# Transposing P by a product with the diagonal of reciprocal sums, in the first twelve units of a fused attention and MLP kernel

## The chip, the core and the metric

The kernel runs on one NeuronCore of one Trainium2 chip. A core has five engines with their own instruction queues: TensorE (PE) for matrix products, VectorE (DVE), ScalarE (ACT), GpSimd (POOL), and SyncE (SP), which here only starts transfers. Each engine works its queue in order. An instruction waits at the head of its queue until what it needs has been signalled by the others, and everything behind it waits with it. The metric is the device time of one execution in microseconds (us). The kernel before took 779.98 us, the median of three runs (778.26 to 780.73).

## The reference

The reference is three steps on float32 data, one after the other: attention with 32 global and 512 local tokens over batch 4 and 8 heads, a gated feed-forward block with a convolution over three tokens, and an FFT mixing block with layer norm and a second feed-forward. The change lies in the local attention of the first step:

```python
s_ll = scale * np.matmul(q_l, k_l.transpose(0, 1, 3, 2))     # 512 x 512 per batch and head
s_ll = np.where(|q - k| <= 32, s_ll, -1e9)
s_lg = scale * np.matmul(q_l, k_g.transpose(0, 1, 3, 2))     # 512 x 32
s_l = np.concatenate([s_lg, s_ll], axis=-1)
e = np.exp(s_l - max)                                        # sm(s)
a_l = e / (np.sum(e, axis=-1, keepdims=True) + 1e-9)
out_l = np.matmul(a_l, np.concatenate([v_g, v_l], axis=2))
```

The weights of the feed-forward block, `w_in` (512 x 1024) and `w_out` (1024 x 512), arrive as float64 bit patterns. The kernel turns each into a pair of 32-bit values, a rounded high part and a low part that is the rest.

## The kernel before

**Units.** Local attention is cut into 32 units. A unit is one pair of heads and one half of the 512 queries of one batch: two heads times two blocks of 128 queries, so four blocks of 128 queries, each against a band of 224 key columns. The steps of unit i, with the names that the order uses:

- `S` (PE): scores of the four blocks, into two PSUM banks.
- `M` (DVE, four): scale, add the mask, take the row's extreme, write the block of P to SBUF (`pb`, 128 x 224 of 256 columns; the last 32 are zero).
- `E` (ACT, four): exponential in place, with the row sums.
- `A` (ACT) and `R` (DVE): add 1e-9 to the four sums, take the reciprocals (`sm`, columns 12 to 15).
- `N` (POOL, four): scale each block of P by its reciprocals, in place (`s_scale`).
- `T` (PE, two halves, one per head): transpose the two blocks of the half, each in two pieces of 128 columns, with `pe.transpose` (`t_mm`).
- `C` (DVE for half 0, ACT for half 1): copy the transposed half to SBUF (`t_evac`).
- `V` (PE): multiply by the values (`pv_mm`), eight products with 64 columns of the values stationary, written alternately to the lower and the upper 64 partitions of the output.
- `XH` (ACT) and `XL` (DVE): the output as a rounded high part and a low part.

Beside them run the global tokens' attention (`GS` to `GXL`), the feed-forward of the first batch (`F`, `H`, `Y`, `TH`, `B`, `D`, where `F` is the product with `w_in` and `D` that with `w_out`), and the making of the sixteen weight tiles, number k of which takes `lw` (SP, load 512 KB), `wa` (ACT, magnitude), `wc` (POOL, clamp), `wt` (ACT) or `wu` (DVE) for the tail bits, `ws` and `wo` (DVE, join and sign), `wh` (ACT, the high part) and `wl` (DVE, the low part, `w_low`).

**Order.** For the first thirteen units the order of all engines is written out by hand in the table `PLAN`: every word is one step, and each engine gets its steps in the order of the words. `PLAN` ends before S13. From unit 13 on, loops give the order on PE and SP, and a scheduler that goes by priorities gives it on the other three engines. Unit 12 has its scores and scaling in `PLAN` and its transposes in the loop.

**Buffers.** P lies in three pairs of `pb` buffers in turn. The transposed halves of units 0, 2, 4 and 6 go to the PSUM banks a2 and a3; those of all others go to the banks s and t, which most scores use too (those of units 1, 3, 5 and 7 use a0 and a1).

Of the kernel before, what the change touches and what calls it, by code (L numbers as in the profile page):

```python
# [42 lines left out]
PLAN = """
lg lq0 lw0 lm1 lq1 li lv0 lw1 S0 lm0 lq2 lc lq3 wu0 wa0 lv1 M0.0 wc0 M0.1 E0.0 M0.2 E0.1 M0.3 S1 ws0 E0.2 E0.3 wo0 A0 lw2 R0 M1.0 wh0 N0.0 lw3 M1.1
E1.0 lq4 wl0 N0.1 E1.1 M1.2 N0.2 M1.3 T0.0 E1.2 E1.3 N0.3 C0.0 wa1 T0.1 wt1 wc1 A1 C0.1 S2 R1 ws1 N1.0 ca wo1 N1.1 V0 lq5 M2.0 wh1 N1.2 M2.1 E2.0 M2.2
wl1 N1.3 E2.1 T1.0 M2.3 E2.2 cd T1.1 E2.3 A2 S3 C1.1 C1.0 wa2 R2 N2.0 V1 wt2 M3.0 M3.1 E3.0 N2.1 M3.2 M3.3 E3.1 N2.2 wu3 lv2 T2.0 XH0 lq6 E3.2 N2.3
XL0 E3.3 C2.0 wc2 T2.1 A3 wa3 R3 S4 ws2 N3.0 C2.1 wo2 N3.1 V2 lw4 M4.0 wh2 N3.2 M4.1 lw5 E4.0 M4.2 N3.3 lw6 wl2 E4.1 T3.0 lw7 M4.3 E4.2 wc3 C3.0 T3.1
E4.3 A4 ws3 S5 C3.1 R4 wo3 wa4 N4.0 V3 M5.0 wh3 N4.1 M5.1 M5.2 E5.0 N4.2 M5.3 E5.1 T4.0 wl3 XH1 N4.3 wu4 E5.2 XL1 wc4 T4.1 E5.3 C4.0 A5 GS0.0 wa5 R5
GS0.1 ws4 C4.1 N5.0 wt5 lq7 GM0.0 N5.1 GM0.1 lv3 wa6 GK0 N5.2 lw8 S6 wo4 wt6 lq8 N5.3 wu7 GE0 V4 lw9 M6.0 wc5 GA0 M6.1 wh4 GR0 wc6 M6.2 E6.0 M6.3 T5.0
E6.1 GN0 wl4 E6.2 T5.1 C5.0 E6.3 F0 ws5 C5.1 wo5 A6 wa7 R6 wa8 ws6 wc7 GT0 wh5 wo6 N6.0 S7 GC0.0 GC0.1 N6.1 wl5 wh6 V5 H0 M7.0 N6.2 wt8 wl6 N6.3 E7.0  # L50
M7.1 F1 M7.2 XH2 wc8 M7.3 E7.1 ws7 E7.2 XL2 E7.3 T6.0 wo7 A7 H1 T6.1 Y0.0 C6.0 F2 wh7 R7 Y0.1 N7.0 C6.1 Y0.2 wa9 N7.1 wl7 GV0 TH0 N7.2 ws8 H2 GS1.0
wt9 N7.3 B0.0 GS1.1 GXH0 GM1.0 B0.1 wc9 GXL0 lq9 Y1.0 GM1.1 lv4 GK1 S8 B0.2 GE1 lw10 wo8 lw11 GA1 Y1.1 Y2.0 lw12 V6 wh8 GR1 lw13 M8.0 GN1 M8.1 lw14
E8.0 M8.2 lw15 F3 E8.1 M8.3 wl8 lq10 E8.2 lq11 E8.3 Y1.2 A8 Y2.1 TH1 T7.0 H3 R8 B1.0 N8.0 T7.1 wa10 C7.0 D0.0 N8.1 C7.1 Y2.2 B1.1 N8.2 D0.1 ws9 wt10
B1.2 N8.3 F4 wa11 wo9 wc10 wt11 wu12 wh9 wc11 ws10 GT1 H4 wl9 TH2 D1.0 GC1.0 GC1.1 B2.0 wa12 D1.1 wo10 B2.1 wc12 wa13 S9 ws11 wh10 wc13 B2.2 wo11 wt13
V7 Y3.0 M9.0 M9.1 E9.0 M9.2 F5 E9.1 M9.3 wl10 XH3 Y3.1 E9.2 E9.3 XL3 T8.0 A9 H5 Y3.2 T8.1 wh11 C8.0 D2.0 TH3 R9 C8.1 wl11 N9.0 D2.1 Y4.0 B3.0 N9.1
wa14 ws12 F6 B3.1 N9.2 wo12 wt14 N9.3 B3.2 wh12 ws13 GV1 wc14 H6 Y5.0 wl12 D3.0 lv5 GXH1 wo13 wa15 lq12 D3.1 GXL1 wc15 wh13 Y4.1 S10 Y4.2 wl13 TH4 V8
B4.0 lq13 M10.0 B4.1 M10.1 E10.0 M10.2 F7 E10.1 M10.3 B4.2 E10.2 Y5.1 E10.3 Y5.2 A10 Y6.0 T9.0 R10 ws14 N10.0 H7 T9.1 TH5 C9.0 N10.1 D4.0 C9.1 wo14
N10.2 D4.1 B5.0 wh14 N10.3 Y6.1 B5.1 F8 wl14 B5.2 Y6.2 Y7.0 D5.0 wu15 H8 TH6 Y7.1 D5.1 B6.0 Y7.2 S11 B6.1 ws15 TH7 B6.2 V9 M11.0 Y8.0 M11.1 E11.0
M11.2 M11.3 E11.1 F9 lv6 B7.0 XH4 lq14 Y8.1 E11.2 XL4 E11.3 T10.0 Y8.2 A11 H9 R11 T10.1 B7.1 wo15 N11.0 TH8 D6.0 C10.0 C10.1 N11.1 wh15 B7.2 D6.1
N11.2 B8.0 Y9.0 wl15 F10 B8.1 N11.3 B8.2 Y9.1 Y9.2 D7.0 H10 TH9 D7.1 Y10.0 B9.0 KA7.0 Y10.1 S12 B9.1 KB7.0 KA7.1 KC7.0 KB7.1 V10 M12.0 M12.1 E12.0  # L60
M12.2 E12.1 M12.3 F11 KC7.1 E12.2 B9.2 E12.3 Y10.2 A12 R12 TH10 T11.0 N12.0 H11 B10.0 T11.1 Y11.0 N12.1 C11.0 B10.1 D8.0 N12.2 C11.1 Y11.1 B10.2 D8.1
N12.3 Y11.2 F12 TH11 B11.0 B11.1 D9.0 B11.2 H12 Y12.0 D9.1 Y12.1 Y12.2
""".split()


# [1339 lines left out]
```

## Time and profile before

| | |
|---|---|
| median of three runs | 779.98 us |
| profiled execution | 780.79 us |
| its span, first to last instruction | 779.0 us |
| PE busy | 756.3 us, 97% |
| DVE busy | 557.4 us, 72% |
| ACT busy | 385.9 us, 50% |
| POOL busy | 157.7 us, 20% |
| chain that ended last | PE 81%, DVE 9%, ACT 7% |

The rows further below come from one profiled execution. Busy time is the time in which an engine had at least one instruction in work. PE's instructions overlap, so the duration of one is longer than the time by which the next follows it; how far apart they start tells more. A float32 product is recorded as two instructions, a transpose as one. In a row, "x<-y" names what is written and what is read, and the time in brackets is how long the engine was idle before it and what ended that. [...]

### The profile page before, as it was taken

What the parts mean: (1) busy time and instruction counts of PE and PEld (TensorE: products, weight loads), DVE (VectorE), ACT (ScalarE), POOL (GpSimd) and SP (SyncE); (2) the same over time, 40 slices, a digit from 0 to 9 for tenths busy, and PEclk for the clock granted to TensorE, in tenths of its full rate; (3) what the DMA queues carried; (4) which work ended last, traced back from release to release, by engine and by line L of the source; (5) the groups of instructions that cost most, each with busy time, mean ns of one, the idle gap of its engine ahead of it and who ended that gap; (6) DMA issues with size and microseconds to landing.
All of it is one profiled execution on the core that took longest, in us unless ns stands there. A gap on an engine that the chain in (4) does not pass through costs nothing.

```text
span 779.0 us, 13835 instructions
## 1 busy us (share of the span) xinstructions
PE 756.3 (97%) x5224; PEld 695.4 (89%) x5224; DVE 557.4 (72%) x1274; ACT 385.9 (50%) x970; POOL 157.7 (20%) x228
## 2 busy tenths in 40 slices
PE   6798999999999999999999999999999999999998
PEld 4587899998989988999898999999999999999997
DVE  5999976778787877799784668876855884545422
ACT  6988767767777766545443265411313421222121
POOL 3755323323223323000223013211100000000000
...
GB/s 312 282 129 177 122 29 76 164 205 73 130 137 178 127 105 117 116 86 252 204 104 0 164 378 84 82 108 121 124 123 0 68 86 137 69 173 76 92 1 46
DMA packets 46594, 98.47 MB, mean 126 GB/s; under 512 B 5224, under 2 KB 26600, under 8 KB 46528
## 3 DMA queue, kind: packets, MB, share of 16 engines
...
## 4 chain that ended last, share of the span: by engine, by line
PE 81%; DVE 9%; ACT 7%; DMA 2%; issue 1%; POOL 0%; SPq 0%; ACTq 0%
PE ps_a L170 29%; PE ps_g L170 20%; PE ps_pv L170 14%; PE ps_s L170 9%; PE ps_t L170 7%; ACT pb L347 3%; DVE y L562 2%; DVE pb L337 1%; DVE mag L660 1%; DMA raw_w<-in_w_out_dram 1%; DMA raw_w<-in_w_in_dram 1%; DVE w_w L677 1%; DVE mag L665 1%; DVE g L582 1%; ACT h L545 1%
## 5 line engine op out<-in xcount | busy, mean ns | idle before, releaser
L170 PE MATMUL ps_g<-x,w_w 128*128 128x256 f32 (+1 forms) x768 | 112.4, 296 | 2.3 <-DVE w_w L677 1.2
L170 PE MATMUL ps_a<-g,w_w 128*128 128x254 f32 (+1 forms) x768 | 113.5, 295 | 1.1 <-DVE g L582 0.6
L170 PEld LDWEIGHTS ps_g<-x,w_w 128*128 128x128 f32 x768 | 101.2, 190 | 8.9 <-issue 3.1
L170 PEld LDWEIGHTS ps_a<-g,w_w 128*128 128x128 f32 x768 | 101.1, 190 | 5.9 <-issue 3.8
L360 POOL TENSOR_SCALAR pb<-pb,sm 128x224 f32<-128x224 f32 x128 | 85.1, 681 | 81.5 <-DVE sm L355 72.6
L170 PE MATMUL ps_a<-hd,w_w 128*128 128x436 f32 (+1 forms) x384 | 81.6, 361 | 0.0
L562 DVE SCALAR_TENSOR_TENSOR y<-h,convw,y 128x254 f32<-128x254 f32 (+1 forms) x128 | 69.1, 541 | 16.3 <-ACT y L558 15.3
L170 PEld LDWEIGHTS ps_a<-hd,w_w 128*128 128x128 f32 x384 | 72.0, 188 | 4.5 <-DVE hd L1200 0.4
L347 ACT ACTIVATE pb<-pb,sm 128x224 f32<-128x224 f32 x128 | 60.4, 473 | 8.2 <-DVE sm L337 7.9
L192 POOL TENSOR_SCALAR mag<-mag 128x512 f32<-128x512 f32 x32 | 25.6, 800 | 178.8 <-ACT mag L191 178.5
L170 PE MATMUL ps_a<-hd,w_v 128*128 128x436 f32 (+1 forms) x288 | 61.0, 360 | 0.0
L170 PEld LDWEIGHTS ps_a<-hd,w_v 128*128 128x128 f32 x288 | 54.2, 188 | 3.0
L1199 ACT ACTIVATE hd<-hh 128x434 fp32r<-128x434 f32 x32 | 18.1, 568 | 59.5 <-DVE hh L1238 30.8
L170 PE MATMUL ps_s<-qk 64*128 64x224 f32 (+1 forms) x144 | 36.5, 406 | 6.9 <-DMA qk<-in_qk_dram 3.6
L567 ACT ACTIVATE y<-y 128x254 f32<-128x254 f32 (+1 forms) x64 | 27.4, 429 | 29.2 <-DVE y L562 29.1
L1200 DVE SCALAR_TENSOR_TENSOR hd<-hh,hd 128x434 fp32r<-128x434 f32 x32 | 19.4, 609 | 30.4 <-ACT hd L1199 30.4
L170 PE MATMUL ps_t<-qk 64*128 64x224 f32 (+1 forms) x144 | 36.3, 403 | 0.0
L227 ACT CAST w_w<-mag 128x512 fp32r<-128x512 f32 x20 | 12.4, 621 | 47.6 <-PE ps_t L170 11.7
L1015 ACT ACTIVATE hd<-ps_g 128x436 fp32r<-128x436 f32 x24 | 12.8, 533 | 46.5 <-PE ps_g L170 46.5
L582 DVE TENSOR_TENSOR g<-y,g 128x254 fp32r<-128x254 f32 (+1 forms) x64 | 28.5, 445 | 9.6 <-ACT g L580 9.6
L545 ACT ACTIVATE h<-ps_g 128x256 f32<-128x256 f32 (+1 forms) x64 | 25.2, 393 | 20.1 <-PE ps_g L170 20.1
L577 DVE SCALAR_TENSOR_TENSOR y<-y,h 128x254 f32<-128x254 f32 (+1 forms) x64 | 28.3, 442 | 9.5 <-ACT y L567 9.2
...
## 6 DMA issues: line engine op xcount, KB each, us to landing
...
```

The lines of the kernel that those rows point to most:

```text
L170: return pe.matmul(o, a, b, start=start, stop=stop)
L192: (clamp or dve).tensor_scalar(mag, mag, TOP, 2.0, op0=ALU.min, op1=ALU.max)
L347: last_exp[0] = act.activation(p, p, AF.Exp, bias=sm[:, k:k + 1], scale=-1.0, accum_out=sm[:, 4 + k:5 + k])
L360: gp.tensor_scalar(pb_of(i, k), pb_of(i, k), sm[:, 12 + k:13 + k], 1.0, op0=ALU.mult, op1=ALU.mult)
L545: act.activation(hbuf[u % NHB][:, h0:h0 + n], h_bank.pop(u), AF.Relu, scale=0.5)
L562: dve.scalar_tensor_tensor(y, o, convw2[:, m, x:x + 1], y, op0=ALU.mult, op1=ALU.add)
L567: act.activation(g_t[u], g_t[u], AF.Tanh, scale=0.5)
L577: dve.scalar_tensor_tensor(y, y, 1.0, hbuf[u % NHB][:, cc:cc + n], op0=ALU.add, op1=ALU.mult)
L582: dve.tensor_sub(gate[u][:, 1], y, f32(gate[u][:, 0]))
L1015: act.activation(hd[:, 0], o, AF.Relu)
L1199: act.activation(hd[:, 0], o, AF.Relu)
L1200: dve.scalar_tensor_tensor(hd[:, 1], o, 0.0, f32(hd[:, 0]), op0=ALU.max, op1=ALU.subtract)
```

## The change

In units 0 to 11 the four scalings `N` are gone. In their place two diagonal matrices per half are made: the identity, times the reciprocals of the rows. A new function `diag` makes both of a half in one instruction of 128 x 256 elements, on POOL (`Qp`, 18 times) or on DVE (`Qd`, units 3 and 8, half 0), or in two instructions on ACT (`Qa`, 4 times). The transposition is then no `pe.transpose` but a product, `turn_scaled`: 64 columns of the unscaled P are stationary, the 128 columns of the diagonal move, and the result is the transposed and scaled piece. Each half takes eight products, alternating between the lower and the upper 64 partitions of the output, where it took four transposes. The diagonals have two buffers in turn, in a tile that uses the space `r0`.

Of the sixteen low parts of weights eleven move from DVE to POOL (`wm`; 1, 2, 4, 6 to 10 and 12 to 14). The tail of weight 0 goes to ACT, and in all there are nine `wt` and seven `wu` where there were ten and six. `PLAN` is written anew; its steps on PE stand in the same order as before.

```diff
@@ PLAN: two of its lines, units 0 and 3 @@
-lg lq0 lw0 lm1 lq1 li lv0 lw1 S0 lm0 lq2 lc lq3 wu0 wa0 lv1 M0.0 wc0 M0.1 E0.0 M0.2 E0.1 M0.3 S1 ws0 E0.2 E0.3 wo0 A0 lw2 R0 M1.0 wh0 N0.0 lw3 M1.1
+lg lq0 lw0 lm1 lq1 lq2 lw1 li S0 lv0 lm0 lc lq3 wa0 lv1 M0.0 wt0 M0.1 wc0 M0.2 E0.0 M0.3 S1 E0.1 ws0 E0.2 wo0 E0.3 lw2 M1.0 A0 lw3 wh0 R0 M1.1 lq4
+S4 A3 wa2 R3 Qd3.0 Qp3.1 wt2 V2 lw6 M4.0 wc2 M4.1 wa3 M4.2 M4.3 T3.0 E4.0 wc3 ws2 E4.1 T3.1 E4.2 C3.0 S5 C3.1 wo2 E4.3 V3 ws3 wh2 A4 wo3 wm2 wa4 R4
...
     def micro():
+        diags = rb.tile([128, 2, 4, 128], F32, tag="r0", name="diags")
+
+        def diag(i, h, eng):
+            o, r = diags[:, i % 2, 2 * h:2 * h + 2], smalls[i][:, 12 + 2 * h:14 + 2 * h]
+            if eng is act:
+                for k in range(2):
+                    act.mul(o[:, k], ident, r[:, k:k + 1])
+            else:
+                eng.tensor_tensor(
+                    o, ident[:, None, :].to_broadcast([128, 2, 128]), r[:, :, None].to_broadcast([128, 2, 128]), op=ALU.mult
+                )
+
+        def turn_scaled(i, h):
+            tb = t_bank[i, h] = bank((("a2", "a3") if solo(i + 1) else ("s", "t"))[h])
+            pb = pbs(i)[h]
+            for a in range(2):
+                for c in range(4):
+                    o = tb[64 * (c % 2):64 * (c % 2) + 64, 256 * (c // 2) + 128 * a:256 * (c // 2) + 128 * a + 128]
+                    mm(o, pb[:, a, 64 * c:64 * c + 64], diags[:, i % 2, 2 * h + a], True, True)
...
-        def w_low(k):
+        def w_low(k, eng=dve):
...
-            dve.tensor_sub(w[:, 1], ring[k % 4], f32(w[:, 0]))
+            eng.tensor_sub(w[:, 1], ring[k % 4], f32(w[:, 0]))
...
-            "T": lambda i, h: t_mm(i, ("a2", "a3") if solo(i + 1) else ("s", "t"), [h]),
+            "Qp": lambda i, h: diag(i, h, gp),
+            "Qa": lambda i, h: diag(i, h, act),
+            "Qd": lambda i, h: diag(i, h, dve),
+            "T": turn_scaled,
...
+            "wm": lambda k: w_low(k, gp),
```

**PE, the transposition of unit 0.** `ident` is the identity, `pb` P, `diags` the diagonals, `qk` the queries and keys. Before, behind the scores of unit 1:

```order
L170 MATMUL ps_a_164<-qk 128x224
L376 MATMUL ps_a_194<-ident,pb_90 128x128
L377 MATMUL ps_a_194<-ident,pb_90 128x128
L376 MATMUL ps_a_194<-ident,pb_90 128x128
L377 MATMUL ps_a_194<-ident,pb_90 128x128
L376 MATMUL ps_a_205<-ident,pb_91 128x128
```

Now, at the same place, up to the scores of unit 2:

```order
L169 MATMUL ps_a_164<-qk 128x224
L169 MATMUL ps_a_197<-diags,pb_90 64x128 x8
L169 MATMUL ps_a_210<-diags,pb_91 64x128 x8
L169 MATMUL ps_s<-qk 128x224
L169 MATMUL ps_t<-qk 128x224
```

Four transposes per half became eight products; nothing else moved on PE, here or later.

**POOL, units 0 to 5.** L647 (now L666) is the clamp of a weight, L360 the scaling of P; L635 is the diagonal, L696 the low part of a weight. Before, from the first clamp on:

```order
L647 TENSOR_SCALAR mag_121<-mag_121 128x512
L360 TENSOR_SCALAR pb_90<-pb_90,sm 128x224 x2
L360 TENSOR_SCALAR pb_91<-pb_91,sm 128x224 x2
L647 TENSOR_SCALAR mag_121<-mag_121 128x512
L360 TENSOR_SCALAR pb_92<-pb_92,sm 128x224 x2
L360 TENSOR_SCALAR pb_93<-pb_93,sm 128x224 x2
```

Now, from the first clamp to unit 5:

```order
L666 TENSOR_SCALAR mag_122<-mag_122 128x512
L635 TENSOR_TENSOR diags<-ident,sm 128x256 x2
L666 TENSOR_SCALAR mag_122<-mag_122 128x512
L635 TENSOR_TENSOR diags<-ident,sm 128x256
L696 TENSOR_TENSOR w_w_250<-mag_122,w_w_250 128x512
L635 TENSOR_TENSOR diags<-ident,sm 128x256 x3
L666 TENSOR_SCALAR mag<-mag 128x512 x2
L696 TENSOR_TENSOR w_w_420<-mag,w_w_420 128x512
L635 TENSOR_TENSOR diags<-ident,sm 128x256
L666 TENSOR_SCALAR mag_122<-mag_122 128x512
L635 TENSOR_TENSOR diags<-ident,sm 128x256 x2
```

The row with `w_w_420` is the low part of weight 2, and the diagonal behind it is that of unit 4, half 0: it stands behind two clamps and a low part.

**SP, the first loads.** `qk` is a unit's queries and keys, `raw_w` a weight, `ident` the identity. Before:

```order
L297 DMA qk<-in_qk_dram 128x608
L206 DMA raw_w_129<-in_w_in_dram 128x4x256
L697 DMA mask<-in_mask_dram 128x448
L297 DMA qk<-in_qk_dram 128x608
L698 DMA ident<-in_ident_dram 128x128
L304 DMA v<-in_v_dram 128x1280
```

Now:

```order
L296 DMA qk<-in_qk_dram 128x608
L205 DMA raw_w_130<-in_w_in_dram 128x4x256
L716 DMA mask<-in_mask_dram 128x448
L296 DMA qk<-in_qk_dram 128x608 x2
L205 DMA raw_w_137<-in_w_in_dram 128x4x256
L717 DMA ident<-in_ident_dram 128x128
L303 DMA v<-in_v_dram 128x1280
```

The third unit's queries and keys and the second weight went ahead of the identity.

## Rows read from the trace of the kernel before

**Rows 1.** Busy us by stretch: PE, PEld, DVE, ACT, POOL; PEclk, DMA share, GB/s.

```profile
3.59:13.51 9.92, 5.89 (x24) 3.52 (x24) 5.74 (x22) 5.92 (x20) 2.88 (x5) 1.00 1.04 375
13.51:42.37 28.86, 24.84 (x186) 18.84 (x185) 25.97 (x83) 24.95 (x75) 18.23 (x29) 0.88 0.72 264
42.37:86.18 43.81, 39.53 (x391) 34.11 (x390) 41.77 (x110) 36.36 (x101) 22.86 (x29) 1.00 0.39 146
86.18:104.85 18.67, 18.67 (x161) 17.47 (x160) 16.53 (x49) 14.03 (x43) 6.04 (x11) 1.00 0.26 90
104.85:779.00 674.15, 667.38 (x4467) 621.44 (x4466) 466.60 (x998) 303.34 (x732) 106.22 (x149) 1.00 0.34 116
```

**Rows 2.** Chain of waits, 95 to 100 us; S12, V10, T11: start, duration, what.

```profile
95.39 0.38 PE ps_s L170
...
96.34 1.03 PE ps_pv L170 x16
...
99.19 0.11 PE ps_s L376
...
99.96 0.11 PE ps_t L377
```

**Rows 3.** PE in order of time: T0, S2, V0, T1, later V11 (start, duration, what).

```profile
11.07 0.47 PE L376 MATMUL ps_a<-ident,pb 128*128 128x128 f32 x1 [0.88 <-POOL pb L360]
...
13.51 0.74 PE L170 MATMUL ps_s<-qk 64*128 64x224 f32 x1
...
15.31 1.97 PE L170 MATMUL ps_pv<-pt,v 128*64 128x128 f32 x16
17.21 0.46 PE L376 MATMUL ps_s<-ident,pb 128*128 128x128 f32 x1
...
105.81 1.10 PE L170 MATMUL ps_pv<-pt,v 128*64 128x128 f32 x16
```

**Rows 4.** Busy time by stretch around the slow clock, columns as above.

```profile
31.00:34.00 3.00, 1.07 (x9) 0.42 (x6) 3.00 (x8) 2.97 (x9) 1.28 (x3) 1.00 0.35 83
34.00:37.60 3.60, 3.60 (x24) 2.63 (x24) 3.56 (x15) 3.57 (x13) 3.42 (x6) 0.58 1.02 412
37.60:40.00 2.40, 2.40 (x13) 2.35 (x12) 1.19 (x2) 0.88 (x4) 0.63 (x1) 0.50 0.89 324
40.00:42.30 2.30, 2.30 (x16) 2.20 (x14) 2.23 (x5) 2.02 (x5) 1.21 (x2) 0.69 0.03 7
```

**Rows 5.** Instructions by line: prices on POOL, DVE and ACT.

```profile
L360 POOL TENSOR_SCALAR pb<-pb,sm 128x224 f32<-128x224 f32 x128 | 85.1, 681 | 81.5 <-DVE sm L355 72.6 <-PE ps_t L377 6.7 <-PE ps_s L377 2.1
L977 POOL TENSOR_TENSOR chl<-cf,chl 128x872 fp32r<-128x872 f32 x2 | 4.1, 2092 | 8.1 <-ACT chl L976 8.1
L984 POOL TENSOR_TENSOR cf<-cf 128x436 f32<-128x436 f32 x1 | 1.1, 1121 | 0.1
...
L677 DVE TENSOR_TENSOR w_w<-mag,w_w 128x512 fp32r<-128x512 f32 x16 | 12.1, 756 | 0.0
L655 DVE TENSOR_SCALAR raw_w<-raw_w 128x512 int32<-128x512 int32 x6 | 3.1, 520 | 5.6 <-DMA raw_w<-in_w_in_dram 5.6
...
L347 ACT ACTIVATE pb<-pb,sm 128x224 f32<-128x224 f32 x52 | 24.5, 473 | 2.3 <-DVE sm L337 2.1
```

**Rows 6.** POOL and DVE in order of time, near 61 us.

```profile
61.14 0.70 POOL L647 TENSOR_SCALAR mag<-mag 128x512 f32<-128x512 f32 x1 [1.06 <-ACT mag L643]
61.28 1.10 DVE L660 SCALAR_TENSOR_TENSOR mag<-mag,raw_w 128x512 int32<-128x512 int32 x1
```

**Rows 7.** The load of the identity: its issue, and us to landing.

```profile
2.67 0.43 SPq L698 DMA_DIRECT2D ident<-in_ident_dram  x1
...
ident<-in_ident_dram SPq DMA_DIRECT2D x1, 64.0 KB, 5.8
```

**Rows 8.** PE's waits to 105 us: in total, times, longest.

```profile
PE ps_s L170 <- DVE smg L440: 1.9, 1, 1.9
PE ps_s L170 <- ACT pgt L489: 1.3, 1, 1.3
```

More of the change, by code (lines that the diff above doesn't have):

```diff
@@ L43 @@
 PLAN = """
-lg lq0 lw0 lm1 lq1 li lv0 lw1 S0 lm0 lq2 lc lq3 wu0 wa0 lv1 M0.0 wc0 M0.1 E0.0 M0.2 E0.1 M0.3 S1 ws0 E0.2 E0.3 wo0 A0 lw2 R0 M1.0 wh0 N0.0 lw3 M1.1
-E1.0 lq4 wl0 N0.1 E1.1 M1.2 N0.2 M1.3 T0.0 E1.2 E1.3 N0.3 C0.0 wa1 T0.1 wt1 wc1 A1 C0.1 S2 R1 ws1 N1.0 ca wo1 N1.1 V0 lq5 M2.0 wh1 N1.2 M2.1 E2.0 M2.2
-wl1 N1.3 E2.1 T1.0 M2.3 E2.2 cd T1.1 E2.3 A2 S3 C1.1 C1.0 wa2 R2 N2.0 V1 wt2 M3.0 M3.1 E3.0 N2.1 M3.2 M3.3 E3.1 N2.2 wu3 lv2 T2.0 XH0 lq6 E3.2 N2.3
-XL0 E3.3 C2.0 wc2 T2.1 A3 wa3 R3 S4 ws2 N3.0 C2.1 wo2 N3.1 V2 lw4 M4.0 wh2 N3.2 M4.1 lw5 E4.0 M4.2 N3.3 lw6 wl2 E4.1 T3.0 lw7 M4.3 E4.2 wc3 C3.0 T3.1
@@ L48 @@
[L48 to L59, printed above, removed]
@@ L60 @@
-N11.2 B8.0 Y9.0 wl15 F10 B8.1 N11.3 B8.2 Y9.1 Y9.2 D7.0 H10 TH9 D7.1 Y10.0 B9.0 KA7.0 Y10.1 S12 B9.1 KB7.0 KA7.1 KC7.0 KB7.1 V10 M12.0 M12.1 E12.0
-M12.2 E12.1 M12.3 F11 KC7.1 E12.2 B9.2 E12.3 Y10.2 A12 R12 TH10 T11.0 N12.0 H11 B10.0 T11.1 Y11.0 N12.1 C11.0 B10.1 D8.0 N12.2 C11.1 Y11.1 B10.2 D8.1
-N12.3 Y11.2 F12 TH11 B11.0 B11.1 D9.0 B11.2 H12 Y12.0 D9.1 Y12.1 Y12.2
+lg lq0 lw0 lm1 lq1 lq2 lw1 li S0 lv0 lm0 lc lq3 wa0 lv1 M0.0 wt0 M0.1 wc0 M0.2 E0.0 M0.3 S1 E0.1 ws0 E0.2 wo0 E0.3 lw2 M1.0 A0 lw3 wh0 R0 M1.1 lq4
@@ new lines @@
+E1.0 M1.2 wl0 E1.1 Qp0.0 wa1 wu1 Qp0.1 M1.3 E1.2 T0.0 E1.3 wc1 C0.0 T0.1 A1 S2 R1 C0.1 ws1 Qp1.1 Qa1.0 wo1 V0 ca lw4 M2.0 lq5 wh1 M2.1 M2.2 E2.0 T1.0
+wm1 M2.3 E2.1 cd T1.1 E2.2 S3 C1.1 C1.0 E2.3 V1 A2 M3.0 R2 M3.1 E3.0 Qp2.0 M3.2 E3.1 M3.3 lv2 Qp2.1 T2.0 XH0 lw5 wu3 E3.2 T2.1 lq6 XL0 E3.3 C2.1 C2.0
+S4 A3 wa2 R3 Qd3.0 Qp3.1 wt2 V2 lw6 M4.0 wc2 M4.1 wa3 M4.2 M4.3 T3.0 E4.0 wc3 ws2 E4.1 T3.1 E4.2 C3.0 S5 C3.1 wo2 E4.3 V3 ws3 wh2 A4 wo3 wm2 wa4 R4
+XH1 M5.0 M5.1 wh3 Qp4.0 XL1 Qa4.1 wc4 wl3 T4.0 wt4 T4.1 M5.2 E5.0 C4.0 GS0.0 C4.1 M5.3 GS0.1 E5.1 GM0.0 E5.2 ws4 lq7 E5.3 lv3 GM0.1 A5 lw7 wa5 GK0 S6
@@ new lines @@
+lw8 R5 wo4 GE0 Qp5.0 lw9 wu5 V4 Qp5.1 lw10 wh4 M6.0 lw11 GA0 M6.1 wc5 wa6 lq8 GR0 M6.2 T5.0 E6.0 M6.3 wm4 ws5 E6.1 T5.1 E6.2 F0 C5.0 GN0 C5.1 wo5 E6.3
+wu6 A6 wh5 R6 wu7 wc6 H0 GT0 wl5 wa7 Qp6.0 S7 GC0.0 GC0.1 ws6 Qp6.1 wa8 V5 wc7 M7.0 wt8 M7.1 E7.0 M7.2 wc8 F1 M7.3 XH2 wo6 E7.1 XL2 E7.2 T6.0 E7.3 ws7
+T6.1 A7 H1 C6.0 wh6 F2 R7 wo7 C6.1 Qp7.0 Y0.0 ws8 Qp7.1 wh7 GV0 wo8 wm6 H2 wa9 GS1.0 Y0.1 GS1.1 GXH0 Y0.2 wm7 wh8 GXL0 lq9 GM1.0 TH0 GM1.1 wt9 lv4 wm8
+GK1 lw12 S8 Y1.0 B0.0 lw13 GE1 wu10 lw14 wc9 Y1.1 V6 lw15 GA1 B0.1 M8.0 lq10 wa10 GR1 M8.1 GN1 F3 M8.2 lq11 E8.0 M8.3 E8.1 B0.2 E8.2 Y1.2 wc10 T7.0
@@ new lines @@
+ws9 E8.3 T7.1 A8 H3 C7.0 TH1 D0.0 R8 C7.1 Qd8.0 Qp8.1 D0.1 B1.0 Y2.0 wo9 B1.1 F4 wa11 B1.2 wh9 Y2.1 wc11 Y2.2 wt11 GT1 wm9 ws10 H4 TH2 D1.0 GC1.1
+GC1.0 B2.0 D1.1 wo10 Y3.0 B2.1 Y3.1 S9 wh10 B2.2 wa12 wm10 Y3.2 V7 wt12 M9.0 M9.1 E9.0 M9.2 wc12 F5 M9.3 E9.1 ws11 XH3 E9.2 wo11 E9.3 T8.0 XL3 A9 T8.1
+H5 C8.0 wh11 D2.0 R9 C8.1 ws12 Qp9.0 D2.1 Qa9.1 wl11 TH3 wa13 wo12 F6 wt13 B3.0 wc13 wu14 B3.1 wh12 ws13 GV1 H6 wm12 B3.2 Y4.0 lv5 wo13 D3.0 GXH1 lq12
+Y5.0 GXL1 wh13 Y4.1 D3.1 Y4.2 wa14 wm13 S10 Y5.1 TH4 Y5.2 wa15 wc14 B4.0 V8 lq13 TH5 M10.0 B4.1 M10.1 wc15 E10.0 M10.2 F7 M10.3 E10.1 B4.2 E10.2 B5.0
@@ new lines @@
+E10.3 ws14 T9.0 A10 H7 R10 T9.1 wo14 B5.1 Qp10.1 Qa10.0 D4.0 C9.0 C9.1 D4.1 B5.2 Y6.0 Y7.0 Y6.1 F8 wh14 Y6.2 wt15 Y7.1 wm14 Y7.2 TH6 D5.0 H8 ws15 TH7
+D5.1 B6.0 B7.0 B6.1 S11 wo15 B7.1 B6.2 wh15 V9 M11.0 Y8.0 M11.1 M11.2 E11.0 M11.3 F9 lv6 XH4 B7.2 lq14 E11.1 Y8.1 E11.2 XL4 T10.0 E11.3 Y8.2 T10.1 A11
+H9 C10.0 D6.0 TH8 R11 C10.1 wl15 Qp11.0 D6.1 Y9.0 B8.0 Qp11.1 Y9.1 B8.1 F10 Y9.2 B8.2 TH9 B9.0 D7.0 H10 Y10.0 D7.1 KA7.0 Y10.1 B9.1 KB7.0 S12 KA7.1
+KC7.0 KB7.1 V10 M12.0 M12.1 E12.0 M12.2 E12.1 M12.3 F11 KC7.1 E12.2 B9.2 E12.3 Y10.2 A12 T11.0 R12 H11 N12.0 TH10 T11.1 C11.0 Y11.0 D8.0 N12.1 B10.0
@@ L63 @@
+C11.1 Y11.1 N12.2 D8.1 B10.1 Y11.2 N12.3 B10.2 F12 TH11 B11.0 B11.1 D9.0 B11.2 H12 Y12.0 D9.1 Y12.1 Y12.2
 """.split()
```

## Prediction, written before the changed kernel was run

> **What bounds the kernel now.** I read the busy time by stretch first, cut where TensorE starts its score products S0, S2, S7, S11 and S13 [rows 1]. The reader is to see four stretches of the part that PLAN orders, and the rest. From 104.85 us on PE is busy for 667.38 of 674.15 us: whatever shifts S13 shifts the end. From 86.18 to 104.85 PE is busy throughout: added PE work costs its full length. From 42.37 to 86.18 DVE is the fuller engine, 41.77 of 43.81 us, and PE stands idle for 4.28. From 13.51 to 42.37 DVE has 25.97 of 28.86, ACT 24.95, and PE is idle for 4.02. So the change is an exchange: PE gets work and DVE loses some, and the question is how much of the PE's idle time before 86 us it can fill.
>
> Then the chain of waits, for what a product costs when PE is the bound [rows 2]: one PV step (V) has eight 64x128 float32 products, recorded as 16, in 1.03 us; the eight transposes of a unit run from 99.19 to 99.96 plus 0.11, so 0.88 us. In time order at the start [rows 3] the same V takes 1.97, and T0 runs from 11.07 to the start of S2 at 13.51, with waits. And the clock [rows 4]: after a stretch in which PE was busy for 1.07 of 3.00 us, the granted clock is 0.58, 0.50 and 0.69 until 42.3.
>
> **The price of a product instead of a transpose.** Each half of a unit becomes eight products with a 64-column stationary P and 128 columns of the diagonal moving: the shape, type and alternation between two column halves of V. The trace does not show this very product. Below, it could cost a unit no more than the transposes, 0.88; above, V with its drain, 2 x 1.10 = 2.20 [rows 3]. I take V inside the chain, the row with the same shape: 2 x 1.03 = 2.06, so 1.18 more a unit, and twelve units make 14.2 us of new PE work at the upper level (2.4 GHz); the far end would add 1.7. PE's order of steps is otherwise the same in both kernels.
>
> **The other engines.** POOL drops 48 scalings of 0.68 (-32.7) and gets 18 diagonals and eleven low parts. A diagonal is a two-input operation of 256 elements: above the one-input scaling of 224 elements, 0.68, below the two-input one of 436, 1.12 [rows 5]; on a line through 436 and 872 elements (1.12 and 2.09) 0.72. I take 0.75. A low part has 512 elements: on the same line 1.29, between 1.12 and 2.09; I take 1.3. Sum +27.8, so POOL does no more than before. DVE loses eleven low parts of 0.756 (-8.3), gains one shift (0.5) and two diagonals of 256 elements, each between nothing and the low part's 0.756 of 512: 0.4. Net -7.0. ACT gains four diagonals of two 128-element scalings, each between nothing and the 0.47 of an exponential of 224: 0.35, so +2.8, and loses a tail. None of the three engines is the bound of the last stretch. In the latency of a unit two scalings (1.36) give way to one diagonal before the first half may be turned.
>
> A two-input DVE operation of 512 elements that ran beside 0.70 us of POOL took 1.10 us [rows 6], 0.34 more than the mean low part. So low parts on POOL may give part of DVE's gain back: 14.3 us of them at that pace cost 7.0 of the 8.3. But the 33 us of scalings that go were on POOL too, so I take no net loss and keep the 7.0 for the range. [...]
>
> **Stretch by stretch.** *To S2.* S1 waits for the same load as before. But the identity, which the diagonal needs, now stands behind two more loads in SP's queue, 304 and 512 KB. Before, it took 5.8 us from an issue at 2.67 [rows 7], so it was there at 8.5; 816 KB at the 375 GB/s of the first stretch are 2.2 us, so it lands at 10.7. The reciprocal is there at about the same time. One diagonal, 0.75, and a hand-over: T0 starts near 11.8 instead of 11.07. [...] So T0's two halves take 2 x 1.9 = 3.8 instead of 2.44. S2 starts at 15.6 instead of 13.51: **+2.1**.
>
> *S2 to S7.* PE was busy for 24.84. Five T cost 5 x 1.18 = +5.9. The lower level from 34 to 42.3 cost 0.42 x 3.6 + 0.5 x 2.4 + 0.31 x 2.3 = 3.4; with PE fed more densely I take it as gone. S2 and V0 ran at the lower level, 3.7 from 13.51 to 17.21 where the chain has 0.95 and 1.03; starting 2.1 later, half of the 1.7 between goes, -0.9. Busy time counts the drain after each run (V alone 1.10, in the chain 1.03); with the waits closed, -1.0. That is 25.4. One wait is new: POOL has the low part of weight 2, which waits for ACT's high part, ahead of unit 4's diagonal. Behind that diagonal stand POOL's clamp and the diagonals of unit 5, and PE's queue waits for it. T4 is late by at least nothing and at most 1.3 + 0.75 = 2.05; as V3 on PE covers part of it, I take 1.5. The longest waits of PE in these two stretches [rows 8], for DVE's reading of the global scores (1.9) and ACT's copy of their transposes (1.3), are DVE and ACT being late; with PE later and DVE lighter I cost them at nothing. 26.9 instead of 28.86: **-1.9**. If the cover is not there, it is the 4.0 of idle time back.
>
> *S7 to S11.* Busy 39.53, four T +4.7, hence 44.2; waits and drains nearly cancel, +0.1 in all: 44.3 instead of 43.81, **+0.5**. DVE has here nine low parts fewer but one moved in, and three joins and a few small steps more, about -3.5: 38.3 of 44.3, so it no longer leads.
>
> *S11 to S13.* Two T, no idle time to fill: **+2.4**.
>
> Sum **+3.1**; behind S13 the order on PE is the same and PE has no idle time, so it stays. The profiled execution took 780.79 (span 779.0 and 1.8 around it), 0.8 above the median of 779.98. On the median: **783.1**.
>
> **Rivals.** *The waits all close.* For: DVE is 7 us lighter and every long PE wait names DVE or ACT. Against: 14.2 us of work must fit into 4.02 + 4.28 us of idle time and 3.4 us of slow clock, and the last stretch has none. Without the T4 wait (-1.5) and with the drains of a fully closed queue in the third stretch (-1.5): +3.1 - 3.0 = +0.1, 780.1. Chance 0.28.
>
> *The clock rises earlier.* Real products in place of transposes might raise the clock before S2 instead of at about 17 us. Then T0 takes 2.06 (-1.7), S2 and V0 run at the upper level (-0.9), and with all waits closed the sum is +0.1 - 2.6 = -2.5: 777.5. For it: in before the pace doubled behind 17.21, after T0, S2 and V0 had run from 11.07 with hardly a break [rows 3]. Against: transposes and products stand mixed there, so the rows cannot say which of them mattered. Chance 0.09. [...]
>
> *The clock falls again (slower).* In before it fell after PE had waited 1.9 us in one piece [rows 4, 8], and stood near half for 8.3 us; a wait of 1.3 did not bring it down. The new wait at T4 is estimated at 1.5, between them. From 1.9 on it decides: 3.4 us for the stretch as before, and the wait itself 0.4 longer: +6.9, 786.9. Chance 0.15.
>
> **How the numbers follow.** Forecast 0.48, rivals 0.28, 0.09 and 0.15. A measurement of this kernel tells 0.3%, 2.3 us, from no change: the bounds around 779.98 are 777.6 and 782.3. The forecast's own spread is 781 to 785.5, of which about a sixth lies under 782.3 (0.07). Faster: the clock rival, 0.09. Same: 0.28 + 0.07 = 0.35. Slower: 0.41 + 0.15 = 0.56. The range goes from 778.5 (waits closed with half the clock gain) to 787.5 (the clock falls, or DVE gives most of its 7.0 back).
>
> **What would show it.** Right: T of a unit fills 2.0 to 2.1 us in the last stretch and S11 to S13 takes 21.0; PE busy throughout from S7; DVE under 39 in the third stretch; S2 near 15.6; a wait of PE on POOL at T4. Wrong: T at 1.5 a unit or less; S7 before 41 or after 45; a granted clock under 1.00 after 20 us; S13 before 105.

## The result, and the profile after

The changed kernel took 786.14 us (median of four, 784.79 to 787.12) and the kernel before, run beside it, 780.36 (778.26 to 781.21): 1.0081 of before, with a 95% interval of 1.006 to 1.0102, so about 6 us slower. The prediction's sign held and its range (778.5 to 787.5) holds the time; its likeliest value, 783.1, is 3 us low.

The profiled execution of after took 787.12, with a span of 785.3 us. It is the slowest of the four; two of them show a mean granted clock of 1.00 and took 784.79 and 785.44. Its busy time by stretch, cut at the starts of S0, S2, S7, S11 and S13 like [rows 1], columns as there (PEclk is the granted clock of TensorE as a share of full speed; the upper and the lower level of the texts read 1.00 and 0.50 in it):

```profile
3.88:13.92 10.04, 7.34 (x49) 5.64 (x49) 6.98 (x25) 6.87 (x22) 3.72 (x5) 1.00 1.06 398
13.92:41.56 27.64, 24.36 (x307) 19.67 (x305) 23.73 (x78) 23.79 (x74) 13.36 (x16) 1.00 0.67 241
41.56:90.98 49.42, 45.42 (x486) 40.08 (x485) 45.80 (x105) 38.69 (x107) 25.55 (x25) 0.93 0.39 143
90.98:112.09 21.11, 21.11 (x210) 19.23 (x209) 17.92 (x50) 14.90 (x44) 3.73 (x9) 1.00 0.23 79
112.09:785.30 673.21, 667.22 (x4467) 621.52 (x4466) 464.42 (x997) 302.95 (x730) 105.10 (x149) 1.00 0.34 117
```

Against [rows 1], S2 comes 0.4 later, S2 to S7 is 1.2 shorter, S7 to S11 is **5.6 longer**, S11 to S13 2.4 longer and the rest 0.9 shorter: 6.3. The reader is to look at DVE in the third row: 105 instructions where there were 110, with eight low parts of weights fewer (two instead of ten), and yet 45.80 us busy where there were 41.77.

PE's waits, 0 to 113 us (in total, times, longest):

```profile
PE ps_s L169 <- DMA qk<-in_qk_dram: 3.9, 1, 3.9
PE ps_a L169 <- POOL diags L635: 3.6, 3, 1.9
PE ps_s L169 <- DVE smg L439: 2.4, 1, 2.4
```

The third one stands ahead of S8. Before has no such wait there: the 1.9 us of [rows 8] stand ahead of S6, for the first group of global tokens.

```profile
33.86 0.64 PE L170 MATMUL ps_s<-qk 64*128 64x224 f32 x2 [1.93 <-DVE smg L440]
```

PE in after, in order of time at S8 (start, duration, what; in brackets the idle time before):

```profile
50.68 0.68 PE L169 MATMUL ps_t<-qk 128*64 128x304 f32 x4
53.72 0.74 PE L169 MATMUL ps_s<-qk 64*128 64x224 f32 x1 [2.36 <-DVE smg L439]
```

DVE at the same place:

```profile
50.25 2.89 DVE L561 SCALAR_TENSOR_TENSOR y<-h,convw,y 128x254 f32<-128x254 f32 x2
53.07 0.21 DVE L514 TENSOR_TENSOR x<-ps_pv,x 128x64 fp32r<-128x64 f32 x1
53.20 0.46 DVE L439 CUSTOM_DVE_ANT_0 sg<-ps_s,gmask 128x304 f32<-128x304 f32 x1
...
53.59 0.46 DVE L439 CUSTOM_DVE_ANT_0 sg<-ps_t,gmask 128x304 f32<-128x304 f32 x1
```

And POOL:

```profile
49.74 4.53 POOL L696 TENSOR_TENSOR w_w<-mag,w_w 128x512 fp32r<-128x512 f32 x3
```

S8 needs the two banks with the second group's scores, which DVE reads at 53.20 and 53.59 (the step GM1). In the new order two convolution steps (Y0.1, Y0.2) stand ahead of these on DVE. Such a step takes 0.47 us by itself; the two take 2.89 here, beside three low parts that run on POOL back to back (why, the experiments show). PE stands idle until 53.72, and then its granted clock is 0.50, and 0.54 from 57.0 on:

```profile
50.60:53.70 3.10, 0.76 (x6) 0.14 (x2) 3.06 (x6) 1.01 (x3) 3.10 (x3) 0.94 0.41 111
53.70:57.00 3.30, 3.28 (x18) 2.68 (x20) 3.27 (x16) 3.27 (x10) 2.15 (x3) 0.50 1.00 393
57.00:60.40 3.40, 3.40 (x22) 2.99 (x18) 1.76 (x5) 1.50 (x7) 0.80 (x2) 0.54 1.05 411
```

The transposition itself, T9 in order of time: by the starts its halves take 0.92 and 0.97 us, so a unit 1.89.

```profile
84.45 1.09 PE L169 MATMUL ps_s<-diags,pb 128*64 128x128 f32 x16 [0.68 <-DVE sm L336]
85.37 1.04 PE L169 MATMUL ps_t<-diags,pb 128*64 128x128 f32 x16
86.34 0.85 PE L169 MATMUL ps_a<-g,w_w 128*128 128x254 f32 x5
```

The transposes of a unit in before, T11, take 0.79 by the same measure, from the first of them to the next product:

```profile
99.03 0.27 PE L376 MATMUL ps_s<-ident,pb 128*128 128x128 f32 x1
...
99.82 1.87 PE L170 MATMUL ps_a<-g,w_w 128*128 128x290 f32 x12
```

### The profile page after: what moved, and what is told of

Read it like the earlier page. It is cut to its first block, busy times and chain, and to the rows that moved or that the text cites. A ratio compares the mean times of both kernels' runs of the same rounds, so it can differ in the third digit from the quotient of the medians.

```text
span 785.3 us, 14378 instructions
## 1 busy us (share of the span) xinstructions
PE 765.5 (97%) x5512; PEld 706.1 (90%) x5512; DVE 559.6 (71%) x1266; ACT 388.5 (49%) x977; POOL 152.9 (19%) x209
## 4 chain that ended last, share of the span: by engine, by line
PE 84%; DVE 8%; ACT 6%; issue 1%; DMA 1%; POOL 1%; SPq 0%; ACTq 0%; POOLq 0%
PE ps_a L169 30%; PE ps_g L169 20%; PE ps_pv L169 14%; PE ps_s L169 10%; PE ps_t L169 8%; DVE y L561 2%; ACT pb L346 2%; DVE mag L679 1%; DVE mag L684 1%; DVE pb L336 1%; DMA qk<-in_qk_dram 1%; DVE y L576 1%; ACT pt L382 1%; ACT h L544 0%; ACT raw_r L193 0%
## 5 line engine op out<-in xcount | busy, mean ns | idle before, releaser
L561 DVE SCALAR_TENSOR_TENSOR y<-h,convw,y 128x254 f32<-128x254 f32 (+1 forms) x128 | 73.5, 576 | 17.4 <-ACT y L557 16.1
L359 POOL TENSOR_SCALAR pb<-pb,sm 128x224 f32<-128x224 f32 x80 | 51.0, 654 | 53.0 <-DVE sm L354 52.2
L191 POOL TENSOR_SCALAR mag<-mag 128x512 f32<-128x512 f32 x32 | 23.3, 728 | 178.8 <-ACT mag L190 178.5
L576 DVE SCALAR_TENSOR_TENSOR y<-y,h 128x254 f32<-128x254 f32 (+1 forms) x64 | 29.9, 469 | 8.0 <-ACT y L566 7.6
L579 ACT CAST g<-y 128x254 fp32r<-128x254 f32 (+1 forms) x64 | 26.5, 416 | 17.3 <-DVE y L576 15.1
```

Of the source, the lines that this page charges most:

```text
L191: (clamp or dve).tensor_scalar(mag, mag, TOP, 2.0, op0=ALU.min, op1=ALU.max)
L561: dve.scalar_tensor_tensor(y, o, convw2[:, m, x:x + 1], y, op0=ALU.mult, op1=ALU.add)
L576: dve.scalar_tensor_tensor(y, y, 1.0, hbuf[u % NHB][:, cc:cc + n], op0=ALU.add, op1=ALU.mult)
L579: act.copy(gate[u][:, 0], y)
```

## The experiments

Three theories stood, A, B and C in the expectations. **Contention** (A): low parts on POOL lengthen DVE's work beside them by more than DVE was relieved. **Price** (B): the products cost 1.0 us a unit wherever they stand. **Order** (C): the new order itself makes PE wait. A run's time is given as a ratio to the kernel before, which took 778.8 us (median) beside each group of these runs; 0.0013 is 1 us. The stretches are read from one profiled execution each, as differences of the starts of S2, S7, S11 and S13:

| kernel | ratio and interval | S2 starts | S2-S7 | S7-S11 | S11-S13 |
|---|---|---|---|---|---|
| before, first trace | 1 | 13.51 | 28.86 | 43.81 | 18.67 |
| before, second trace | 1 | 11.84 | 25.77 | 45.21 | 18.67 |
| after | 1.0081 [1.006, 1.0102] | 13.92 | 27.64 | 49.42 | 21.11 |
| after, again | 1.0101 [1.0081, 1.0121] | 14.13 | 28.07 | 49.79 | 21.10 |
| products only | 1.0023 [1.0012, 1.0035] | 13.11 | 26.10 | 44.00 | 21.10 |
| low parts only | 1.0047 [1.0034, 1.0059] | 12.01 | 26.50 | 47.67 | 19.57 |
| after, low parts back | 1.0071 [1.0054, 1.0087] | 13.79 | 27.34 | 45.50 | 21.10 |
| after, transposes back | 1.0100 [1.0086, 1.0115] | 14.12 | 29.92 | 47.68 | 19.96 |
| after, GM1 first | 1.0087 [1.0073, 1.0101] | 14.71 | 27.79 | 47.38 | 21.10 |
| after, two places, low parts back | 1.0053 [1.0035, 1.0071] | 15.17 | 26.97 | 45.77 | 21.10 |
| products in units 0 to 6 | 1.0003 [0.9991, 1.0015] | 15.25 | 26.08 | 44.43 | 18.67 |
| products in units 0 to 9 | 1.0011 [1.0001, 1.0022] | 13.88 | 26.75 | 44.70 | 18.69 |
| before, POOL + 11, two inputs | 1.0073 [1.0058, 1.0089] | 11.94 | 28.08 | 49.83 | 19.31 |
| before, POOL + 11, one input | 1.0069 [1.0054, 1.0084] | 12.01 | 27.03 | 49.74 | 19.34 |

The two traces of before differ by 3.1 us in S2 to S7 and by 1.4 in S7 to S11; a difference of that size between two single traces tells little.

### The parts, each alone

Products only: order and low parts of before, `N` replaced in units 0 to 11, all diagonals on POOL.

```diff
-N0.0 ... N0.1 ... N0.2 ... N0.3 ... T0.0
+Qp0.0 ... Qp0.1 ... T0.0
```

> The order and the low parts of before, with the transposition alone changed in units 0 to 11: diagonals on POOL (two instructions a unit), eight products a half. Theory A (the loss comes mainly from low parts on POOL, which stretch DVE's operations with two inputs from SBUF): the added PE work shows, about 2.4 us from S11 to S13 and little elsewhere; 2 to 4 us over before, and mean DVE durations of the convolution step L561 and of the sign step stay near those of before (0.5 and 0.76 us). Theory B (the loss is the price of the products, 1.0 us a unit in twelve units, and the order and the low parts win some back): 5.8 us over before or more. Theory C (the newly written order costs): close to A, and less than half of the change's +5.8.

Measured: 1.0023, 1.8 us over before, just under what contention and order expected. From S11 to S13 the products cost 2.4, as in after. From S7 to S11 they cost nothing:

```profile
39.21:83.21 44.00, 42.84 (x487) 37.72 (x486) 43.30 (x110) 37.12 (x102) 17.58 (x20) 1.00 0.41 148
83.21:104.31 21.10, 21.10 (x210) 19.22 (x209) 17.47 (x50) 14.86 (x44) 4.40 (x9) 1.00 0.24 80
```

PE is busy for 42.84 there instead of 39.53, in as long a stretch: idle time was filled. The price theory falls.

Low parts only: order, scalings and transposes of before.

```diff
-wl1 ... wl2 ... wl4 ... wl6 wl7 wl8 wl9 wl10 ... wl12 wl13 wl14
+wm1 ... wm2 ... wm4 ... wm6 wm7 wm8 wm9 wm10 ... wm12 wm13 wm14
```

> The order, the scalings and the transposes of before, with the eleven low parts moved from DVE to POOL at their places in the order. Theory A: DVE's operations beside them grow; DVE busy from S7 to S11 stays over 40 us in spite of nine low parts fewer, and the time is 1 to 4 us over before. Theory B: DVE is lighter by up to 8.3 us, PE's waits on it close; 2 to 5 us under before. Theory C: no change within 0.3%, since the order is that of before.

Measured: 1.0047, 3.7 us over before. DVE has fewer instructions from S7 to S11, again two low parts instead of ten, and is busy for longer than in [rows 1] (41.77) and in the second trace of before (43.63):

```profile
38.51:86.18 47.67, 39.91 (x390) 34.05 (x389) 44.35 (x102) 37.41 (x104) 34.02 (x38) 1.00 0.39 143
```

That is what contention expected (over 40 us), with the order unchanged.

The two crossed with the new order:

```diff
@@ low parts back: the changed kernel @@
-wm1 ... wm14
+wl1 ... wl14
@@ transposes back: the changed kernel @@
-Qp0.0 ... Qp0.1
+N0.0 N0.1 ... N0.2 N0.3
-            "T": turn_scaled,
+            "T": lambda i, h: t_mm(i, ("a2", "a3") if solo(i + 1) else ("s", "t"), [h]),
```

> The changed kernel with its eleven low parts back on DVE, at the same places in the new order. Theory A: the wait of 2.4 us ahead of S8 and the lower clock behind it go; the sign and convolution steps of DVE take 0.76 and 0.5 us again; 2 to 5 us under the changed kernel. Theory B: DVE gets 8.3 us more and leads from S7 to S11; 0 to 3 us over the changed kernel. Theory C: as the changed kernel, within 0.3%.

Measured: 1.0071. The lower clock behind S8 is not in this trace (1.00 from S7 to S11), but the wait ahead of S8 is 2.0 us still, so the first part of what contention expected fails: most of that wait belongs to the order.

```profile
52.77 0.64 PE L169 MATMUL ps_s<-qk 64*128 64x224 f32 x2 [2.01 <-DVE smg L439]
```

In the chain of single steps before (1), products (1.0023), new order with its places for the diagonals (1.0071), low parts on POOL (1.0101) the new order is worth 3.7 us, the products 1.8 and the low parts 2.3. The last two intervals just meet, at 1.0081 to 1.0087, and against after's first result the low parts are worth only 0.8, the "within 0.3%" of the order theory. The shares also depend on the path: with low parts first (1.0047), the new order next (1.0100, transposes back, below) and products last (1.0101), the low parts are worth 3.7, the order 4.1 and the products nothing. So the new order costs about 4 us on either path, and the rest is not split by these runs. What says more of the low parts is S7 to S11, 45.50 against 49.42 and 49.79, and DVE in it, less busy with eight low parts more:

```profile
41.13:86.63 45.50, 42.68 (x487) 37.59 (x486) 44.66 (x114) 39.44 (x109) 13.52 (x17) 1.00 0.43 156
```

> The changed kernel with the transposes and the four scalings a unit on POOL back, the low parts and the rest of the order as changed. Theory A: the stretch of DVE remains, with POOL fuller still; the last two units take 18.7 us again (2.4 less), the time is 1 to 3 us under the changed kernel and still over before. Theory B: 6 us under the changed kernel or more, so at before or under it. Theory C: 2 to 3 us under the changed kernel.

Measured: 1.0100, no better than after, a miss of all three. The last two units come back by only 1.1 us, and up to S7 it loses: POOL now has four scalings of a unit and the low parts, PE waits for the scalings 5.0 us in all, 3.0 at the longest, and the mean granted clock of the execution is 0.996. In this order four scalings a unit cost PE more waiting than two diagonals do (3.6 us in after).

### Two waits of the new order

> The changed kernel once more, on the same chip as the next three and in more executions. Every theory: 5.5 to 7.5 us over before, with the wait of about 2.4 us ahead of S8 on DVE's global scores; the time scatters by some 2 us with how long the lower clock lasts behind it.

Measured: 1.0101. Of six executions four show a mean granted clock of 0.993 to 0.995 and took 787.5 to 788.5, two show 1.00 and took 784.6 and 785.5.

```diff
@@ GM1 first: the changed kernel @@
-GS1.0 Y0.1 GS1.1 GXH0 Y0.2 wm7 wh8 GXL0 lq9 GM1.0 TH0 GM1.1
+GS1.0 GS1.1 GM1.0 GM1.1 Y0.1 GXH0 Y0.2 wm7 wh8 GXL0 lq9 TH0
@@ two places, low parts back: GM1 as above, wl for wm, and for unit 4 @@
-wo2 E4.3 V3 ws3 wh2 A4 wo3 wl2 wa4 R4 XH1 M5.0 M5.1 wh3 Qp4.0 XL1 Qa4.1
+wo2 E4.3 A4 V3 ws3 R4 Qp4.0 wh2 Qa4.1 wo3 wl2 wa4 XH1 M5.0 M5.1 wh3 XL1
```

> The changed kernel with one edit of order: the two readings of the global scores (GM1) stand on DVE ahead of the two convolution steps Y0.1 and Y0.2, not behind them. Order theory (the new order has two places where PE waits for DVE's queue, of which this is the longer): the 2.4 us wait ahead of S8 falls below 0.7, the lower clock behind it goes, 2 to 4 us under the changed kernel. Contention theory (low parts on POOL stretch DVE, and DVE leads from S7 to S11): DVE has the same work in the same stretch, so the wait comes back at a later place; 0 to 1 us under the changed kernel.

Measured: 1.0087, 1.1 us under after, the intervals overlapping. S8 waits no more, S7 to S11 is 2.4 shorter than in the second trace of after, at a granted clock of 1.00 throughout, but the wait came back behind S8, at PV:

```profile
PE ps_pv L169 <- DVE x L514: 1.6, 1, 1.6
```

DVE's work did not change (45.55 of 47.38 us), so this fits contention: DVE leads, and where PE meets it is a matter of order. The 2 to 4 us that the order theory expected did not come. All six executions took 785.6 to 786.1; the four of after whose mean clock is 1.00 took 784.6 to 785.5. So the edit spares after the 1.4 to 3.9 us that its executions with a mean clock of 0.993 to 0.996 lose, though two of its own six show 0.995 too, and gains nothing more.

> The changed kernel with its low parts back on DVE, GM1 ahead of the two Y, and unit 4's reciprocal and diagonals ahead of the joins and the high part that stood before them. Order theory: these two waits (2.0 and 1.7 us) are what the new order cost beside the products, so the time falls by 2 to 3.5 us from the kernel with the low parts back (4.9 over before) to 1.5 to 3 us over before, as the products alone. If the order costs by its many small shifts instead: 4 to 5 us over before.

Measured: 1.0053, 4.1 us over before, as the second expectation had it; against 1.0071 it is a gain of 1.4 us, within the intervals. So the order theory holds for the sum (3.7 us) and not for these two waits: some 2.3 us of the new order remain against products only. Which places of the order cost them is not shown.

### What POOL does to DVE

Eleven instructions more on POOL in the kernel before, whose result nothing reads, one behind each place of a moved low part:

```diff
+        spare = rb.tile([128, 8, 128], F32, tag="r0", name="spare")
+        def extra(_):    # two inputs
+            eye = ident[:, None, :].to_broadcast([128, 4, 128])
+            gp.tensor_tensor(spare[:, 0:4], eye, eye, op=ALU.mult)
+        def extra(_):    # one input, in the other run
+            eye = ident[:, None, :].to_broadcast([128, 8, 128])
+            gp.tensor_scalar(spare, eye, TOP, 2.0, op0=ALU.min, op1=ALU.max)
```

> The kernel before, with eleven instructions more on POOL whose result nothing reads: the identity times itself, 512 elements, two inputs, one behind each place of the eleven low parts. DVE's work is that of before. Contention theory: DVE's all-SBUF operations beside them take up to three times their length; DVE's busy time from S7 to S11 stays near full, and this stretch grows by 2 to 5 us; 2 to 4 us over before. If POOL's operations do not hold DVE up: within 1 us of before, since POOL has 20 us of idle time in that stretch.

> The control of the run with two inputs: eleven instructions on POOL with one input and 1024 elements, about as long (1.2 to 1.4 us). If it is POOL's second input that holds DVE up: within 1 us of before. If any POOL work does, or if it is POOL's queue that is late with the scalings: 2 to 4 us over before, like the other.

Measured: 1.0073 and 1.0069, 5.7 and 5.4 us over before. DVE has exactly its old work and is busy for 48.76 and 48.02 us where the second trace of before has 43.63. With two inputs:

```profile
40.02:89.85 49.83, 43.37 (x391) 37.06 (x390) 48.76 (x111) 38.05 (x104) 36.55 (x39) 0.93 0.38 139
```

With one input:

```profile
39.04:88.78 49.74, 43.35 (x390) 37.04 (x389) 48.02 (x111) 38.31 (x104) 36.53 (x39) 0.93 0.38 138
```

So it is not POOL's second input. It could be POOL's queue, late with the scalings; but PE's waits for these grew only from 2.0 us in the second trace of before to 2.9 (two inputs). The granted clock of the stretch is 0.93 in both traces, but that is not the main part: two executions with two inputs show a mean clock of 1.00 and took 783.45 and 785.07, still 4.7 and 6.3 us over before. One pair in order of time shows what happens. With one input, DVE:

```profile
87.16 1.25 DVE L562 SCALAR_TENSOR_TENSOR y<-h,convw,y 128x254 f32<-128x254 f32 x1
88.34 0.41 DVE L661 TENSOR_SCALAR raw_w<-raw_w 128x512 int32<-128x512 int32 x1
```

and POOL:

```profile
87.05 1.09 POOL L632 TENSOR_SCALAR spare<-ident 128x1024 f32<-128x1024 f32 x1
```

POOL ends at 88.14, DVE at 88.41, 0.27 later. Low parts only, DVE:

```profile
84.55 1.50 DVE L562 SCALAR_TENSOR_TENSOR y<-h,convw,y 128x254 f32<-128x254 f32 x1
```

and POOL:

```profile
84.33 1.45 POOL L697 TENSOR_TENSOR w_w<-mag,w_w 128x512 fp32r<-128x512 f32 x1
```

POOL ends at 85.78, DVE at 86.05: 0.27 again. The step, 0.47 by itself, does not run slower; it **waits until the POOL instruction in work has ended**, so the more of that one is left, the longer the wait. These pairs are no choice: in the first 115 us of the fourteen traces 84 steps of this shape start while a POOL instruction on a tile is in work, and every one ends 0.26 to 0.29 after it, though its length goes from 0.45 to 1.72. After's three low parts and two Y [the DVE and POOL rows at S8 above] show the same in turns: the third low part starts at 52.83, when the second has ended, and the second Y ends at 53.14. DVE's reading of the scores from PSUM at 53.20, which ran beside the third low part, took 0.46, no longer than the 0.48 and 0.47 of the readings at 33.48 and 34.49 with no POOL instruction in work, and the steps M, which read PSUM too, take 0.36 to 0.40 in all these traces, beside POOL or not: these steps with an input from PSUM were not held.

### Where products cost nothing

The order, low parts and scalings are those of before; the line is shown against the changed kernel.

```diff
-            "T": turn_scaled,
+            "T": lambda i, h: turn_scaled(i, h) if i < 7 else t_mm(i, ("a2", "a3") if solo(i + 1) else ("s", "t"), [h]),
```

> Order, low parts and scalings of before, with products and diagonals in units 0 to 6 only. If a product costs only where PE has no idle time (the last two stretches) and is free or a gain before S7, where it lets T start after one diagonal and PE reaches the upper clock earlier: 0.5 to 2.5 us under before, the last two units take 18.7 us again. If the 1.9 us of products alone came from all stretches alike: 1 us over before.

Measured: 1.0003, between the two expectations, no change that can be told. The last two units are at 18.67 again.

> Order, low parts and scalings of before, with products and diagonals in units 0 to 9. From S7 to S11 PE has idle time that three more products can fill: as the kernel with units 0 to 6, between 1 us under and 0.5 over before, S7 to S11 near 44.0 us, the last two units at 18.7. If products cost their length there too: 2 to 3 us over before.

Measured: 1.0011, 0.9 us over before, just outside what was expected. PE is busy for 43.01 of 44.70 us from S7 to S11, 2.6 more than with units 0 to 6, and the stretch is 0.3 longer: nearly free, but no gain either. No version here beats the kernel before.

> The kernel before once more, for a second trace of it. If the lower clock of its first trace (34 to 42 us) is no steady part of it, this trace may show a granted clock of 1.00 throughout; then S2 to S7 takes 25.5 to 26.5 us instead of 28.86, and the profiled time is 777.5 to 778.7 us. If it is steady, 28 to 29 us again.

Measured: 778.26 us, span 776.5, clock 1.00 in every stretch:

```profile
11.84:37.61 25.77, 21.07 (x186) 15.39 (x186) 23.97 (x82) 23.66 (x74) 17.34 (x27) 1.00 0.82 299
37.61:82.82 45.21, 39.66 (x390) 34.36 (x389) 43.63 (x111) 37.64 (x104) 24.57 (x30) 1.00 0.41 152
82.82:101.49 18.67, 18.67 (x161) 17.48 (x161) 16.53 (x49) 14.02 (x43) 6.06 (x11) 1.00 0.26 90
101.49:776.50 675.01, 667.74 (x4467) 621.46 (x4466) 466.39 (x998) 303.76 (x732) 106.47 (x149) 1.00 0.34 116
```

The lower clock of [rows 4] was no steady part of the kernel before: of its 17 executions in one group of runs 13 show a mean granted clock of at least 0.999 (median 778.29), three 0.992 to 0.995 (780.27 to 781.34).

## Why the prediction was partly right

The time lies inside the range in part by luck: against the first trace of before S7 to S11 and S2 to S7 came 5.1 and 0.7 us over the sum, and the start of S2 and the rest behind S13 1.7 and 0.9 under it.

**The price of a product: right.** Forecast 2.06 a unit, 1.18 over the transposes; by the starts 1.89, 1.10 over them, and S11 to S13, with two units, grew by 2.44 against 2.4. That PE's idle time before S11 can take them up held too: alone, they fill 3.3 us more of S7 to S11 at no cost. No run shows the 2.4 GHz that the forecast puts beside its 14.2 us: the traces give the granted clock as a share of full speed, 1.00 from S11 to S13 in before and after, and that stretch grew by the 2.44.

**S7 to S11, +0.5: the step that failed.** It measured +5.6 against the first trace and +4.2 against the second. Of the 5.4 us between products only (44.00) and after (49.42), 1.5 come with the new order (45.50), 1.9 more with the low parts while the clock stays up (47.38, GM1 first), and 2.0 with the wait at S8 and the clock behind it. Each is a difference of single traces, so the split is rough. Two things in the sum were wrong.

- *"I take no net loss"* on DVE, and so *"38.3 of 44.3, so it no longer leads"*. DVE was busy for 45.80 and led. With eight low parts fewer it was 1.1 us busier than with them back (44.66), not 6 us lighter (eight times 0.756). [Rows 6] already showed the waiting: POOL's clamp ended at 61.84, and DVE's join beside it at 62.38, 0.54 later. The prediction read the 1.10 as a slower pace, spread it as 0.34 per instruction, and set the scalings that go against the low parts that come, by their sum on POOL (33 us against 14). But the price of a meeting is what is left of the POOL instruction: the scalings are short (0.68) and the low parts long (1.47), and DVE's convolution steps stand beside them. The sum of busy time on POOL does not say what is left at a meeting.
- *A wait that the sum has no term for.* The two waits that it did *"cost at nothing"* went, as it said: the 1.9 us ahead of S6 is 0.35 in after, and the 1.3 for ACT's copy is gone. But PE waits 2.4 us ahead of S8, where before waits 0.3 at most (second trace), because the new order puts two Y ahead of GM1 on DVE, behind low parts on POOL. DVE's new order was at hand; the prediction followed the orders of PE, POOL and SP.

Of its own signs, a granted clock under 1.00 after 20 us, named as one of being wrong, came, and DVE under 39 us did not; S7 at 41.56 and S11 to S13 at 21.11 were as forecast.

**S2 to S7, -1.9: right in sign, for a reason that was none.** Forecast 26.9, measured 27.64. The sum took 3.4 us of lower clock as gone for good. It was gone, but most executions of before don't have it: against the second trace the stretch is 1.9 longer, not 1.2 shorter. The new wait at T4 was seen (1.94 us, forecast 1.5), and only part of it is POOL's low part: with that back on DVE it is 1.72, since the reciprocal of unit 4 stands behind steps of the weights on DVE.

**To S2, +2.1: half right.** S1 to S2 takes 6.7 us instead of 5.2, but not because the identity is late: T0 began at 10.31, before the 11.8 of the forecast, and ran 3.6 us, near the forecast's 3.8. That 3.8 was the author's estimate, by the pace of V in [rows 3]: V0 took 1.97 there and V11 1.10, although the granted clock reads 1.00 at both (from 13.51 to 17.21 us and behind 104.85). In after the sixteen products of T0 took 3.68, and those of T9 1.09 and 1.04 by halves, so the slow pace at the start is there; no run shows a frequency for it. S1 itself started at 7.18 instead of 8.32, by when its load landed; this start lies between 6.7 and 8.6 in the traces of all these kernels. Against the second trace of before S2 does come 2.1 later, but 0.4 of that is S1's start: the agreement is chance.

**Behind S13, nothing: 0.9 off.** The first trace of before has a wait of PE in the FFT step that after has not; why is left open. The stretch from S13 to the end lies between 672.9 and 675.0 in the fourteen traces.

```profile
389.53 1.39 PE L170 MATMUL ps_t<-s,ab 92*128 92x274 f32 x9 [0.94 <-DVE u L898]
```

**The rivals.** *The clock falls again* came closest (786.9), but its place was wrong: at T4 a wait of 1.94 did not bring it down in the first trace of after (1.00 from S2 to S7) and did for a moment in the second (0.67 from 30 to 34 us); at S8 2.4 did in both (0.50 from 53.7 to 57 us in the first, 0.50 from 58 to 62 in the second). *The waits all close* did not come: PE still stands idle for 4.0 us from S7 to S11. *The clock rises earlier*: in after the PV step V0 takes 1.10 from 15.71, with products ahead of it, and in the second trace of before 1.19 from 13.64, with transposes; in the first trace of before it took 1.97 from 15.31 [rows 3], with transposes too. No effect of the kind of instruction can be seen.
